# A routed expert layer on one core: room for 608 rows per expert in place of 640

## The chip, the cores and the metric

The kernel runs on one core of a Trainium2 chip. The metric is the time of one execution on the device in microseconds (us). A profiled execution has a span as well, from its first to its last instruction, and it is always a little shorter than that execution's time. TensorE (PE) multiplies, VectorE (DVE), ScalarE (ACT) and GpSimd (POOL) work on rows of 128 partitions, and SyncE (SP) issues most of the transfers.

## The reference

Three layers follow each other on 2304 tokens of width 512.

```python
# 1: attention through 32 memory slots, 4 x 8 heads, 576 tokens, head size 64 -> x (2304, 512)
# 2: mixture of experts, N, D, E, F = 2304, 512, 8, 1024
top2 = np.argpartition(-noisy_logits, 2, axis=1)[:, :2]
...
for e in range(E):
    for k in range(2):
        mask = top2[:, k] == e
        h = np.maximum(x[mask] @ w1[e], 0.0)
        out[mask] += top2_w[mask, k, None] * (h @ w2[e])
# 3: x @ w_in -> g = h * cos(h) -> g @ w_out, inner width 2048
```

Each token goes to two of the eight experts, so 4608 rows are spread over the experts, and how many each one gets depends on the inputs.

## The kernel before

**Stages.** The attention comes first, 18 tiles of 128 tokens. Then come the eight experts, one after the other, and then the last layer, again by tiles of tokens. All large products are made from pairs of half-precision numbers (a high part and a low part of each operand), so each product is three matmuls: high by high, high by low, low by high.

**Room.** Each expert has a fixed room of `CAP` = 640 rows, `NST` = 5 tiles of 128. The rows of the first eight token tiles (the first group, routed early) fill the first two tiles (`CA` = 2). All others go to the second group, tiles 2 to 4. When the first group gives an expert fewer than 256 rows, its two tiles are filled up, so the rows an expert uses are the larger of 256 and its first-group count, plus its second-group count. Rows that no longer fit are left to the function `overflow`, a loop over further tiles of 128 rows with a count `nov` that is computed on the chip (`slots_`). The loop reads the count from a register, stands between the first and the second product of the last expert, and runs zero times when every expert fits.

**One expert.** `gather_x` fetches an expert's rows from the table `xd` in DRAM, one indirect transfer for a tile of 128 rows (`xg`), and a transposing transfer puts them in `xT` (named x in the rows). `l1(e, part, f)` is the first product for block f of the inner width: 12 matmuls, whose moving operand is as wide as the part, 256 columns in the first and 384 in the second. `l1_out` writes the rectified result as high part on ACT and low part on DVE (hT). `l2(e, c)` is the second product for tile c: 24 matmuls with a piece of hT as stationary operand and 512 columns of weights moving. `l2_out` scales the tile on ACT (o) and stores it in the table `yd`. Expert 7 makes its products in another order than the rest: first part, tiles 0 and 1, second part, tiles 2 to 4.

**Work beside the experts.** The 16 weight matrices (index 2e and 2e + 1 for expert e) are loaded as f32 (raw), squared and summed on ACT (junk) for a scale, and split into high and low parts (w) on ACT and DVE. The weights of the last layer arrive as 64-bit floats in 16 chunks, are converted on DVE and ACT (cvt, cvu), and stored to `wst` in DRAM, from where `load_win` and `load_wout` read them back. The column sums for the scales are small matmuls on PE (sums).

**Order.** A planner writes everything in one list, `line`. Each entry has a planned time, and the list is sorted by it and issued. `put_l1` and `put_l2` advance a planned clock by `d1` and `d2` and note when ACT and DVE have room (`free`). `put_weights` and `put_chunk` take the next free slots, first come first served. Instructions of one engine keep the order in which they were issued (`chain`), and a second list (`settle`) does the same for the last layer, planned back from `m0`, the end of the expert stage.

Of the kernel before, what the change touches and what calls it, by code (L numbers as in the profile page):

```python
# [11 lines left out]
F32 = mybir.dt.float32  # L12
# [4 lines left out]
AF = mybir.ActivationFunctionType  # L17
OP = mybir.AluOpType
# [3 lines left out]
P = 128  # L22
# [3 lines left out]
DM = H * D  # L26
E = 8
F = 1024
DFF = 2048
CAP = 640  # L30
NST = CAP // P
GROUPS = [(0, 8), (8, 18)]
NA = GROUPS[0][1]
NG = NT - NA
ROUTE_OF = [g for g, (a, b) in enumerate(GROUPS) for t in range(a, b)]
CA = 2
MAXOV = 26
Y0 = MAXOV * P
YROWS = Y0 + E * CAP
TB = N // 4  # L40
# [22 lines left out]
def fused_kernel(ctx, tc, phiT, qT, kv, wgn, noise, w1, w2, wi, wo, out):  # L63
    nc = tc.nc
    V, A, G, T, SP = nc.vector, nc.scalar, nc.gpsimd, nc.tensor, nc.sync

    xd = nc.dram_tensor("xd", (N, 2 * DM), F16).ap()
    yd = nc.dram_tensor("yd", (YROWS, DM), F32).ap()
# [99 lines left out]
    def l2k(shape, dt, name):  # L168
        return lp.tile(shape, dt, tag="l", name=name)
# [27 lines left out]
    ecap = sm([P, E], F32, "ecap")  # L197
    G.iota(ecap, pattern=[[CAP, E]], base=0, channel_multiplier=0, allow_small_or_imprecise_dtypes=True)
    ekey = sm([P, E], F32, "ekey")
# [83 lines left out]
    def chain(key, fn, *a, **kw):  # L283

        with gated(key):
            last[key] = fn(*a, **kw)  # L286
# [87 lines left out]
    ne = base[1]  # L374
# [8 lines left out]
    def rt(name, shape, dt=F32):  # L383
        return small.tile(shape, dt, tag="r" + name, name="r" + name)
# [139 lines left out]
    def slots_():  # L524

        ti = rt("oi", [P, E], I32)
        cnt = rt("ocnt", [P, E])
        V.tensor_scalar(cnt, ne, float(-CAP), 0.0, op0=OP.add, op1=OP.max)
        V.tensor_scalar(ti, cnt, 127.0, None, op0=OP.add)
        V.tensor_scalar(ti, ti, 7, None, op0=OP.arith_shift_right)  # L530
        V.tensor_copy(cnt, ti)
        ca, cb = rt("oca", [P, E]), rt("ocb", [P, E])
        V.tensor_copy(ca, cnt)
        for s in (1, 2, 4):
            V.tensor_copy(cb[:, :s], ca[:, :s])
            V.tensor_tensor(cb[:, s:], ca[:, s:], ca[:, :E - s], op=OP.add)
            ca, cb = cb, ca
        cinc, cexc = ca, rt("oce", [P, E])
        V.tensor_tensor(cexc, cinc, cnt, op=OP.subtract)
        V.tensor_copy(nov, cinc[:, E - 1:E])  # L540
        corr, corr4 = rt("ocorr", [P, E]), rt("ocr4", [P, E])
        V.scalar_tensor_tensor(corr, cexc, float(P), ecap, op0=OP.mult, op1=OP.subtract)
        V.tensor_scalar(corr, corr, float(-CAP - Y0), None, op0=OP.add)
        yield
        ge, sl = rt("g", [P, NT, E]), rt("ocm", [P, NT, E])
        pos = key
        V.tensor_scalar(corr4, ecap, -4096.0 / CAP, None, op0=OP.mult)
        V.tensor_tensor(pos, key, bc_e(corr4, NT), op=OP.add)
        V.tensor_scalar(ge, pos, float(CAP), None, op0=OP.is_ge)
        V.tensor_tensor(ge, ge, bc_e(corr, NT), op=OP.mult)  # L550
        V.scalar_tensor_tensor(sl, pos, float(Y0), bc_e(ecap, NT), op0=OP.add, op1=OP.add)
        V.tensor_tensor(sl, sl, ge, op=OP.add)
        yield
        sf = rt("osf", [P, NT, 2])
        for k in range(2):
            V.tensor_tensor(ge, sl, oh[k], op=OP.mult)
            V.tensor_reduce(sf[:, :, k], ge, axis=AX.X, op=OP.add)
        V.tensor_copy(sidx, sf)
        yield
        uf = rt("ouf", [P, MAXOV])  # L560
        G.iota(uf, pattern=[[1, MAXOV]], base=0, channel_multiplier=0, allow_small_or_imprecise_dtypes=True)
        cm = rt("ocm", [P, MAXOV, E])
        ef, of = rt("oef", [P, MAXOV]), rt("oof", [P, MAXOV])
        V.tensor_tensor(cm, bc_t(uf, MAXOV), bc_e(cinc, MAXOV), op=OP.is_ge)
        V.tensor_reduce(ef, cm, axis=AX.X, op=OP.add)
        V.tensor_tensor(cm, bc_t(uf, MAXOV), bc_e(cexc, MAXOV), op=OP.is_ge)
        V.tensor_tensor(cm, cm, bc_e(cexc, MAXOV), op=OP.mult)
        V.tensor_reduce(of, cm, axis=AX.X, op=OP.max)
        V.tensor_tensor(of, uf, of, op=OP.subtract)
        V.tensor_scalar(ef, ef, float(E - 1), None, op0=OP.min)  # L570
        V.tensor_copy(ue, ef)
        V.scalar_tensor_tensor(ua, ef, 32.0, of, op0=OP.mult, op1=OP.add)
        V.tensor_scalar(ua, ua, float(NST), None, op0=OP.add)

    slot_steps = slots_()

# [298 lines left out]
    def bank_y():  # L875
        return turns("y", (("kt", 1), ("ya", 0), ("yb", 0)))
# [6 lines left out]

    xT, hT, prod = {}, {}, {}
    parts = [(0, CA), (CA, NST)]

    xg = {}

# [16 lines left out]
        chain("load", SP.dma_start_transpose, out=xT[e, part][:, :, (c - c0) * P:(c - c0 + 1) * P], in_=xg[e, c])  # L905

    def l1(e, part, f):
        c0, c1 = parts[part]
        n = (c1 - c0) * P
        if f == 0:  # L910
            if part == 0:
                h = hs("hT", 0, [P, 2, 8, n], F16)
                hT[e, part] = h[:, 0], h[:, 1]
            else:
                hT[e, part] = tuple(hs("hT", 0, [P, 8, n], F16) for w in range(2))
        x = xT[e, part]
        ph = prod[e, part, f] = bank_h()
        w = wt[2 * e]
        for k in range(4):
            fs = slice(k * F + f * P, k * F + (f + 1) * P)  # L920
            with gated("rank" if f else f"t{NT - 1}P") if (e, part, k) == (0, 0, 0) and f in (0, 2) else nullcontext():
                chain("P", T.matmul, ph[:, :n], lhsT=w[:, 0, fs], rhs=x[:, k, :], start=(k == 0), stop=False)
            chain("P", T.matmul, ph[:, :n], lhsT=w[:, 0, fs], rhs=x[:, 4 + k, :], start=False, stop=False)
            chain("P", T.matmul, ph[:, :n], lhsT=w[:, 1, fs], rhs=x[:, k, :], start=False, stop=(k == 3))

    def l1_out(e, part, f):
        n = (parts[part][1] - parts[part][0]) * P
        hi, lo = hT[e, part]
        ph = prod.pop((e, part, f))
        chain("A", A.activation, hi[:, f, :], ph[:, :n], AF.Relu)  # L930
        with gated("m161") if (e, part, f) == (0, 0, 0) else nullcontext():
            chain("V", V.scalar_tensor_tensor, lo[:, f, :], ph[:, :n], 0.0, hi[:, f, :], op0=OP.max, op1=OP.subtract)

    def l2(e, c):
        part = 0 if c < CA else 1
        cs = slice((c - parts[part][0]) * P, (c - parts[part][0] + 1) * P)
        hi, lo = hT[e, part]
        w = wt[2 * e + 1]
        py = prod[e, c] = bank_y()
        for f in range(8):  # L940
            ws = slice(f * DM, (f + 1) * DM)
            chain("P", T.matmul, py, lhsT=hi[:, f, cs], rhs=w[:, 0, ws], start=(f == 0), stop=False)
            chain("P", T.matmul, py, lhsT=hi[:, f, cs], rhs=w[:, 1, ws], start=False, stop=False)
            chain("P", T.matmul, py, lhsT=lo[:, f, cs], rhs=w[:, 0, ws], start=False, stop=(f == 7))
# [17 lines left out]

    def l2_out(e, c):
        py = prod.pop((e, c))
        o = l2k([P, DM], F32, "o")
        chain("A", A.activation, o, py, AF.Copy, scale=ysc[:, e:e + 1])
        r0 = Y0 + e * CAP + c * P
        chain("A", A.dma_start, yd[r0:r0 + P, :], o)

    def overflow():  # L970

# [254 lines left out]
              zero[0][:, None, :].to_broadcast([P, 2, DM]))  # L1226


    d1, d2 = (1.31, 1.95), 5.18
    xe = 8 * sum(d1) + NST * d2  # L1230
    X = [a_end + 0.5]
    at(tA + 0.0094, next_pools)
    at(tA, gather_x, 0, 0, lead=LA)
# [153 lines left out]
    def put_weights(i, t_load, t_sq, t_hi):  # L1387
        for h in range(2):
            at(t_load[h], w_load, i, h)
        for c in range(4):  # L1390
            t_sq = slot(t_sq)
            at(t_sq, w_square, i, c)
        t = max(t_hi, put_scale(t_sq + 2.0, i, 4) + 1.5)
        for c in range(4):
            t = slot(t)
            at(t, w_hi, i, c)
            at(t + 1.2, w_lo, i, c)
# [3 lines left out]
    def put_chunk(c, t):  # L1401
        t = max(t, stored.get(c - 2, 0.0) + 4.0)
        at(t, c_load, c)
        t = slot(t + 9.0)
        at(t, c_abs, c)
        for k in range(4):
            at(t + 0.8 + 1.8 * k, c_bits, c, k)
        t = slot(t + 9.0)
        at(t, c_square, c)
        t = slot(put_scale(t + 2.0, 2 * E + c, 1) + 1.5)  # L1410
        at(t, c_hi, c)
        at(t + 1.2, c_lo, c)
        stored[c] = t + 4.0
        at(stored[c], c_store, c)

    OV, LP, PRE = 13.0, 16.0, 30.0
    x = X[E - 2]
    put_weights(2 * E - 1, (x + 12.0, x + 15.0), x + 27.0, 0.0)
    for c in range(2 * NCH):
        put_chunk(c, X[1] + 2.0 + 18.5 * c)  # L1420
    put_weights(2, (tA - 12.0, tA + 0.0001), X[0] + 1.0, 0.0)
    put_weights(3, (X[0] + 4.0, X[0] + 8.0), X[0] + 17.0, X[1] + 1.5)
    for e in range(2, E):
        x = X[e - 1]
        put_weights(2 * e, (x - 6.0, x - 3.0), x + 11.5, 0.0)
        if e < E - 1:
            put_weights(2 * e + 1, (x + 12.0, x + 15.0), x + 30.0, 0.0)
    for k in range(4):
        at(X[1] + 8.0 + 6.0 * k, slots)
    for u in range(0, MAXOV, 2):  # L1430
# [47 lines left out]
```

## Time and profile before

| | |
|---|---|
| median of 3 runs | 913.83 us (912.25 to 913.85) |
| the profiled execution | 912.87 us, span 911.1 us |
| mean granted TensorE clock | 0.977 of full speed |
| PE busy | 874.9 us, 96% of the span |
| DVE, ACT, POOL busy | 586.4, 468.8, 213.5 us |
| chain that ended last | PE 86%, DVE 4%, issue 4%, ACT 2%, DMA 2% |

The attention takes the first 105 us, the experts follow to 530 us, the last layer takes the rest. The chain that ended last is the profile's own path back from the last instruction, through whatever released each step. Idle time of an engine that is off that path costs nothing by itself.

### The profile page before, as it was taken

The page shows a single profiled execution, that of the slowest core. Times are in us where ns is not written, and L with a number is a line of the kernel's source. Part 1 is how long each engine was busy: PE and PEld are TensorE (multiplying, and loading weights), DVE is VectorE, ACT ScalarE, POOL GpSimd, SP SyncE. Part 2 cuts the span into 40 slices and gives each one's busy share as a digit, 9 for nine tenths or more (in the row PEclk, how much of TensorE's full clock was granted, in tenths as well). Part 3 has the DMA queues.
Part 4 walks back from the last instruction along what each step waited for, and adds up shares of the span by engine and source line. Part 5 has one row for each costly group of instructions (what it writes and reads, how often), then busy time and mean ns, then how long its engine had stood idle before and what let it go on. Part 6 is the DMA issues. An engine that isn't in the chain of part 4 may idle for free.

```text
span 911.1 us, 14175 instructions
## 1 busy us (share of the span) xinstructions
PE 874.9 (96%) x5368; PEld 509.5 (56%) x5368; DVE 586.4 (64%) x1267; ACT 468.8 (51%) x830; POOL 213.5 (23%) x234
## 2 busy tenths in 40 slices
PE   5997499999999999999999999999999999999997
PEld 4875355756556474656646566664444444444564
DVE  3668753776658575775762469999878645455564
ACT  4688426566666676777772344454433322322233
POOL 1355222110200101020000145442632222122221
PEclk9897599999999999999999999999999999999999
DMA  9982459887868979698656534240512102100001
GB/s 350 395 322 83 115 157 248 258 282 255 236 252 257 266 225 310 234 280 329 188 178 216 140 133 115 59 104 24 139 47 47 47 1 24 46 1 1 1 24 47
DMA packets 108406, 146.55 MB, mean 161 GB/s; under 512 B 65840, under 2 KB 66736, under 8 KB 106288
## 3 DMA queue, kind: packets, MB, share of 16 engines
q1 hardware_dynamic: 89840, 103.95, 37.0%
q0 software_dynamic: 6080, 19.93, 7.5%
q10 hardware_dynamic: 12416, 21.74, 6.6%
q8 instruction: 43, 0.70, 0.3%
q14 instruction: 27, 0.22, 0.1%
HBM read 95.26 MB, written 35.13 MB: 143 GB/s over the span
## 4 chain that ended last, share of the span: by engine, by line
PE 86%; DVE 4%; issue 4%; ACT 2%; DMA 2%; POOL 1%; ACTq 0%; SPq 0%; POOLq 0%; DVEq 0%
PE h L286 22%; PE y L286 22%; PE g L286 19%; PE o L286 18%; PE x L756 1%; DVE tt L286 1%; PE kp L656 1%; PE sc L726 1%; DMA kvt<-in_kv 1%; DVE ty L286 1%; ACT tt L286 1%; POOL xg L896 1%; DMA xg<-xd,idxB 0%; ACT o L286 0%; PE sums L286 0%
## 5 line engine op out<-in xcount | busy, mean ns | idle before, releaser
L286 PE MATMUL h<-x,w 128*128 128x384 f16 (+1 forms) x1536 | 215.1, 301 | 9.1 <-DMA x<-xg 8.7
L286 PE MATMUL y<-w,hT 128*128 128x512 f16 x960 | 210.5, 379 | 0.0
L286 PE MATMUL g<-x2T,win 128*128 128x256 f16 (+1 forms) x1152 | 202.2, 326 | 0.0
L286 PE MATMUL o<-wout,gT 128*128 128x512 f16 x864 | 201.5, 379 | 0.0
L286 PEld LDWEIGHTS <-w 128*128 128x128 f16 x1536 | 151.5, 99 | 68.0 <-DMA x<-xg 8.8
L286 PEld LDWEIGHTS <-win 128*128 128x128 f16 x1152 | 112.7, 98 | 83.9
L286 PEld LDWEIGHTS <-hT 128*128 128x128 f16 x960 | 93.9, 99 | 109.0
L286 POOL TENSOR_TENSOR gT<-ty,gT 128x256 f16<-128x256 f32 (+1 forms) x96 | 90.9, 947 | 246.2 <-ACT gT L286 246.0
L286 ACT ACTIVATE tt<-tt,hp 128x256 f32<-128x256 f32 (+1 forms) x96 | 59.0, 614 | 156.0 <-DVE tt L286 149.7
L286 PEld LDWEIGHTS <-gT 128*128 128x128 f16 x864 | 84.6, 98 | 91.8
L286 DVE SCALAR_TENSOR_TENSOR hT<-h,hT 128x384 f16<-128x384 f32 (+1 forms) x128 | 61.6, 486 | 77.4 <-ACT hT L286 77.2
L286 DVE SCALAR_TENSOR_TENSOR w<-raw,wsc,w 128x1024 f16<-128x1024 f32 x64 | 81.0, 1286 | 32.8 <-ACT w L286 32.7
L286 DVE SCALAR_TENSOR_TENSOR ty<-g,wis,bct 128x256 f32<-128x256 f32 (+1 forms) x96 | 58.8, 612 | 66.3 <-PE g L286 64.2
L286 ACT ACTIVATE hT<-h 128x384 f16<-128x384 f32 (+1 forms) x128 | 55.5, 435 | 75.9 <-PE h L286 72.5
L286 DVE SCALAR_TENSOR_TENSOR ty<-g,fac,tt 128x256 f32<-128x256 f32 (+1 forms) x96 | 59.0, 615 | 45.0 <-ACT tt L286 44.3
L286 ACT ACTIVATE gT<-ty 128x256 f16<-128x256 f32 (+1 forms) x96 | 50.2, 523 | 62.2 <-DVE ty L286 60.9
L896 POOL DMA_INDIRECT xg<-xd,idxB x24 | 25.4, 1058 | 218.2 <-DMA x<-xg 206.9
L286 ACT ACTIVATE w<-raw,wsc 128x1024 f16<-128x1024 f32 x64 | 71.7, 1140 | 4.7 <-ACT o L286 2.1
L286 DVE SCALAR_TENSOR_TENSOR tt<-tt,ty 128x256 f32<-128x256 f32 (+1 forms) x96 | 69.6, 725 | 3.0
L286 ACT ACTIVATE junk<-raw 128x1024 bf16<-128x1024 f32 x64 | 67.3, 1052 | 3.9 <-ACT o L286 3.4
L286 ACT ACTIVATE o<-y,ysc 128x512 f32<-128x512 f32 x40 | 27.5, 687 | 67.3 <-PE y L286 66.2
L286 POOL DMA_INDIRECT y<-yd,sidx x36 | 35.2, 979 | 86.5 <-DMA yd<-o 79.3
(235 smaller groups left out, 710.2 us busy)
## 6 DMA issues: line engine op xcount, KB each, us to landing
raw<-in_w SPq DMA_DIRECT2D x32, 1024.0 KB, 8.7
yd<-o ACTq DMA_DIRECT2D x40, 256.0 KB, 5.6
kvt<-in_kv SPq DMA_DIRECT2D x9, 1024.0 KB, 15.5
cvt<-in_wi SPq DMA_DIRECT2D x8, 1024.0 KB, 6.5
wst<-cvt SPq DMA_DIRECT2D x16, 512.0 KB, 3.6
cvt<-in_wo SPq DMA_DIRECT2D x8, 1024.0 KB, 8.8
yd<-zero ACTq DMA_DIRECT2D x13, 512.0 KB, 5.4
xd<-hl SPq DMA_DIRECT2D x18, 256.0 KB, 2.0
```

Of the source, the lines that this page charges most:

```text
L286: last[key] = fn(*a, **kw)
L656: T.matmul(kp[32 * j:32 * j + 32, g, :], lhsT=es[i][:, 32 * h:32 * h + 32], rhs=kvv[:, :, h * D:(h + 1) * D], start=(i == 0), stop=(i == 4))
L726: T.matmul(sc[p0:p0 + n, 64 * c:64 * c + 64], lhsT=qt[t // 8][:, c, c0:c0 + n], rhs=bdkt[b][:, c, :], start=True, stop=True)
L756: last[f"t{t}P"] = T.matmul(x[pn, g, 0:272], lhsT=eT[:, g, pn], rhs=bdv[b][:, g, :], start=True, stop=True)
L896: G.indirect_dma_start(out=g, out_offset=None, in_=xd[0:NA * P] if part == 0 else xd, in_offset=bass.IndirectOffsetOnAxis(ap=idx[:, col:co ...
```

## The change

The room becomes 608 rows: still five tiles, of which the fifth has 96 rows. The first product of the second group moves 352 columns in place of 384, its two output steps work on 352 columns, the second product of tile 4 has 96 stationary columns, and its output and store have 96 rows. Gathers and transposes keep all 128 rows of a tile. An expert with more than 608 rows hands its whole fifth tile, and all beyond, to the loop (`FULL` = 512), for which room is made for 28 tiles in place of 26. The planner is told of 1.80 us for a block of the second group in place of 1.95, it spaces the 16 chunks 17.8 us apart in place of 18.5, and the second weights of expert 7 take their slots after all other weights and chunks, no longer before.

```diff
-CAP = 640
-NST = CAP // P
+CAP = 608
+NST = -(-CAP // P)
+FULL = (NST - 1) * P
...
-MAXOV = 26
+MAXOV = 28
...
-        V.tensor_scalar(cnt, ne, float(-CAP), 0.0, op0=OP.add, op1=OP.max)
-        V.tensor_scalar(ti, cnt, 127.0, None, op0=OP.add)
+        V.tensor_scalar(ti, ne, float(P - 1 - FULL), 0.0, op0=OP.add, op1=OP.max)
         V.tensor_scalar(ti, ti, 7, None, op0=OP.arith_shift_right)
         V.tensor_copy(cnt, ti)
+        V.scalar_tensor_tensor(cnt, ne, CAP + 0.5, cnt, op0=OP.is_ge, op1=OP.mult)
...
+    width = (CA * P, CAP - CA * P)
...
     def l1(e, part, f):
-        c0, c1 = parts[part]
-        n = (c1 - c0) * P
+        n = width[part]
...
-        x = xT[e, part]
+        x = xT[e, part][:, :, :n]
...
     def l1_out(e, part, f):
-        n = (parts[part][1] - parts[part][0]) * P
+        n = width[part]
...
     def l2(e, c):
         part = 0 if c < CA else 1
-        cs = slice((c - parts[part][0]) * P, (c - parts[part][0] + 1) * P)
+        m = min(P, CAP - c * P)
+        cs = slice((c - parts[part][0]) * P, (c - parts[part][0]) * P + m)
...
-        py = prod[e, c] = bank_y()
+        py = prod[e, c] = bank_y()[:m]
...
     def l2_out(e, c):
         py = prod.pop((e, c))
-        o = l2k([P, DM], F32, "o")
-        chain("A", A.activation, o, py, AF.Copy, scale=ysc[:, e:e + 1])
+        m = min(P, CAP - c * P)
+        o = l2k([P, DM], F32, "o")[:m]
+        chain("A", A.activation, o, py, AF.Copy, scale=ysc[:m, e:e + 1])
         r0 = Y0 + e * CAP + c * P
-        chain("A", A.dma_start, yd[r0:r0 + P, :], o)
+        chain("A", A.dma_start, yd[r0:r0 + m, :], o)
...
-    d1, d2 = (1.31, 1.95), 5.18
+    d1, d2 = (1.31, 1.80), 5.18
...
-    x = X[E - 2]
-    put_weights(2 * E - 1, (x + 12.0, x + 15.0), x + 27.0, 0.0)
     for c in range(2 * NCH):
-        put_chunk(c, X[1] + 2.0 + 18.5 * c)
+        put_chunk(c, X[1] + 2.0 + 17.8 * c)
...
+    x = X[E - 2]
+    put_weights(2 * E - 1, (x + 12.0, x + 15.0), x + 27.0, 0.0)
```

On ACT the place that changes most is the end of expert 6 and the start of expert 7. In the order before, these are its instructions from the first conversion of expert 7's second weights (w_4866, from raw_4612 and raw_4651); w_4776 are its first weights, o and the store to yd belong to tiles of expert 6, and hT 128x256 is expert 7's first product.

```order
L286 ACTIVATE w_4866<-raw_4612,wsc_113 128x1024
L286 ACTIVATE o_4870<-y_4829,ysc_115 128x512
L286 DMA yd<-o_4870 128x512
L286 ACTIVATE w_4866<-raw_4612,wsc_113 128x1024
L286 ACTIVATE w_4866<-raw_4651,wsc_113 128x1024 x2
L286 ACTIVATE o_4906<-y_4873,ysc_115 128x512
L286 DMA yd<-o_4906 128x512
L286 ACTIVATE junk_859,wmx_109<-cvu_4687 128x1024
L286 ACTIVATE w_4776<-raw_4438,wsc_113 128x1024
L286 ACTIVATE o_4938<-y_4909,ysc_115 128x512
L286 DMA yd<-o_4938 128x512
L286 ACTIVATE hT_4941<-h_4942 128x256
```

In the changed program the second weights are called w_4938, the first ones w_4777, and from their first conversion on ACT has this.

```order
L287 ACTIVATE w_4938<-raw_4613,wsc_113 128x1024
L287 ACTIVATE o_4941<-y_4906,ysc_115 96x512
L287 DMA yd<-o_4941 96x512
L287 ACTIVATE hT_4944<-h_4945 128x256
L287 ACTIVATE hT_4944<-h_4964 128x256
L287 ACTIVATE w_4938<-raw_4613,wsc_113 128x1024
L287 ACTIVATE hT_4944<-h_4979 128x256
L287 ACTIVATE w_4938<-raw_4652,wsc_113 128x1024
L287 ACTIVATE hT_4944<-h_4996 128x256
L287 ACTIVATE w_4938<-raw_4652,wsc_113 128x1024
L287 ACTIVATE hT_4944<-h_5013 128x256
```

Three of the four conversions of expert 7's second weights have moved from before its first product to between the blocks of it, and the last piece of its first weights no longer stands just ahead of expert 6's last tile.

On SP's queue the place is the end of the expert stage, behind the loop. In the order before: chl_5526 and chl_5573 are token tiles 0 and 1 of the last layer, x2T is where they are transposed to, and wout_5619 is the first half of the last layer's second weights.

```order
L286 DMA wout_5425<-wst 128x2x2048
L286 DMA wout_5427<-wst 128x2x2048
L286 DMA_TRANSPOSE x2T_5545<-chl_5526 128x8x128
L286 DMA_TRANSPOSE x2T_5545<-chl_5573 128x8x128
L286 DMA wout_5619<-wst 128x4x2048
```

The same place of the changed program, where tile 1 is chl_5589:

```order
L287 DMA wout_5426<-wst 128x2x2048
L287 DMA wout_5428<-wst 128x2x2048
L287 DMA_TRANSPOSE x2T_5546<-chl_5527 128x8x128
L287 DMA wout_5619<-wst 128x4x2048
L287 DMA_TRANSPOSE x2T_5546<-chl_5589 128x8x128
```

The transpose of token tile 1 now stands behind the large load of wout.

## Rows read from the trace of the kernel before

**Rows 1.** Stages: us; PE, PEld, DVE, ACT, POOL busy (instructions); PEclk, DMA share, GB/s.
```profile
105.10:162.15 57.05, 56.45 (x337) 33.19 (x338) 25.34 (x74) 24.81 (x43) 12.37 (x13) 0.95 0.70 198
214.90:530.30 315.40, 315.40 (x1924) 188.25 (x1923) 190.63 (x334) 197.48 (x311) 29.55 (x27) 1.00 0.77 241
530.30:911.10 380.80, 375.58 (x2033) 199.00 (x2031) 265.57 (x529) 142.86 (x248) 121.39 (x127) 1.00 0.18 47
```
**Rows 2.** PE's waits, longest in total first (us, times, longest).
```profile
PE h L286 <- DMA x<-xg: 8.7, 1, 8.7
...
PE h L286 <- DVE hT L286: 0.2, 1, 0.2
```
**Rows 3.** Groups of PE matmuls by shape: busy us, mean ns of one, idle before.
```profile
L286 PE MATMUL h<-x,w 128*128 128x384 f16 x768 | 127.1, 326 | 0.1
L286 PE MATMUL h<-x,w 128*128 128x256 f16 x768 | 88.9, 277 | 9.0 <-DMA x<-xg 8.7 <-DVE hT L286 0.2
```
**Rows 4.** PE's timeline, expert 2: start us, us, instruction, count.
```profile
214.90 10.64 PE L286 MATMUL h<-x,w 128*128 128x256 f16 x96
225.38 0.28 PE L286 MATMUL sums<-wmx,ones 128*128 128x2 f32 x2
225.52 15.76 PE L286 MATMUL h<-x,w 128*128 128x384 f16 x96
241.12 0.28 PE L286 MATMUL sums<-wmx,ones 128*128 128x5 f32 x2
241.26 5.34 PE L286 MATMUL y<-w,hT 128*128 128x512 f16 x24
246.44 0.28 PE L286 MATMUL sums<-wmx,ones 128*128 128x2 f32 x2
```
**Rows 5.** Groups of PE's weight loads by shape.
```profile
L286 PEld LDWEIGHTS <-hT 128*128 128x128 f16 x960 | 93.9, 99 | 109.0
...
L286 PEld LDWEIGHTS sums<-wmx,ones 128*128 128x128 f32 x64 | 11.5, 194 | 4.8 <-ACT junk L286 2.0
```
**Rows 6.** ACT's timeline in the second group of expert 6.
```profile
440.15 0.49 ACT L286 ACTIVATE hT<-h 128x384 f16<-128x384 f32 x1 [0.42 <-PE h L286]
...
442.10 0.49 ACT L286 ACTIVATE hT<-h 128x384 f16<-128x384 f32 x1 [0.42 <-PE h L286]
```
**Rows 7.** Groups of ACT and DVE by shape: weights, and the first group's output.
```profile
L286 ACT ACTIVATE w<-raw,wsc 128x1024 f16<-128x1024 f32 x64 | 71.7, 1140 | 4.7 <-ACT o L286 2.1 <-DVE wsc L286 1.9 <-issue 0.6
...
L286 ACT ACTIVATE hT<-h 128x256 f16<-128x256 f32 x64 | 24.3, 380 | 35.7 <-PE h L286 32.3 <-PE tab L500 3.4
...
L286 DVE SCALAR_TENSOR_TENSOR w<-raw,wsc,w 128x1024 f16<-128x1024 f32 x64 | 81.0, 1286 | 32.8 <-ACT w L286 32.7
...
L286 DVE SCALAR_TENSOR_TENSOR hT<-h,hT 128x256 f16<-128x256 f32 x64 | 26.5, 418 | 19.3 <-ACT hT L286 19.3
```
**Rows 8.** SP's and PE's timelines where the last layer begins, and x2T's transposes.
```profile
514.53 10.52 PE L286 MATMUL y<-w,hT 128*128 128x512 f16 x48
...
530.29 6.71 PE L286 MATMUL g<-x2T,win 128*128 128x256 f16 x60
...
L286 SPq DMA_TRANSPOSE x2T<-chl x2: 1232/1317/1402, 511.5 to 517.9; - x2
...
519.18 0.53 SPq L286 DMA_DIRECT2D wout<-wst  x1
```
**Rows 9.** Transfers from 494 to 560 us: count, KB each, us from issue to landing.
```profile
wout<-wst SPq DMA_DIRECT2D x1, 2048.0 KB, 9.3
...
x2T<-chl SPq DMA_TRANSPOSE x4, 3.2
```
**Rows 10.** Work like that of one turn of the loop.
```profile
raw<-in_w SPq DMA_DIRECT2D x32, 1024.0 KB, 8.7
...
xg<-xd,idxB POOLq DMA_INDIRECT x24, 6.7
...
L498 DVE TENSOR_SCALAR ohp<-iota_r,pf x36: 235/241/548, 86.2 to 118.9; 128x128 f16<-128x128 f16 x36
```

More of the change, by code (lines that the diff above doesn't have):

```diff
@@ L542, in slots_ @@
         V.scalar_tensor_tensor(corr, cexc, float(P), ecap, op0=OP.mult, op1=OP.subtract)
-        V.tensor_scalar(corr, corr, float(-CAP - Y0), None, op0=OP.add)
+        V.tensor_scalar(corr, corr, float(-FULL - Y0), None, op0=OP.add)
         yield
@@ L546, in slots_ @@
         pos = key
-        V.tensor_scalar(corr4, ecap, -4096.0 / CAP, None, op0=OP.mult)
+        V.tensor_scalar(corr4, ekey, 4096.0, -4096.0 * E, op0=OP.mult, op1=OP.add)
         V.tensor_tensor(pos, key, bc_e(corr4, NT), op=OP.add)
@@ L572, in slots_ @@
         V.scalar_tensor_tensor(ua, ef, 32.0, of, op0=OP.mult, op1=OP.add)
-        V.tensor_scalar(ua, ua, float(NST), None, op0=OP.add)
+        V.tensor_scalar(ua, ua, float(NST - 1), None, op0=OP.add)
     slot_steps = slots_()
@@ L1226, in clear @@
               zero[0][:, None, :].to_broadcast([P, 2, DM]))
-    d1, d2 = (1.31, 1.95), 5.18
-    xe = 8 * sum(d1) + NST * d2
+    d1, d2 = (1.31, 1.80), 5.18
     X = [a_end + 0.5]
```

## The prediction

> **What bounds the kernel now.** I read the stages first, then PE's waits, then PE's timeline, because the whole gain of this change can only come from PE.
>
> The stages [rows 1]: from 214.90 to 530.30 us PE is busy for 315.40 of 315.40 us at full clock, while DVE has 190.63 and ACT 197.48. PE is the limit of the expert stage, with a third of the time free on the other two. In the last stage PE has 375.58 of 380.80 us. A busy PE alone would not prove it, since a matmul that waits inside its pipeline could look busy, so the waits and the spacings come next.
>
> PE's waits [rows 2]: the long one, 8.7 us for the first transposed rows of expert 0, lies before the changed work begins. The other wait on the expert stage's list is 0.2 us for hT. From the first product on nothing holds PE up.
>
> The spacings [rows 4]: 96 matmuls of 256 columns take 225.38 - 214.90 = 10.48 us, 109.2 ns each. 96 of 384 columns take 241.12 - 225.52 = 15.60 us, 162.5 ns each. 24 of 512 columns take 246.44 - 241.26 = 5.18 us, 215.8 ns each. (The mean ns of the groups [rows 3] is the length of one pipelined matmul and not what one costs.) From 256 to 384 columns a column costs 53.3 / 128 = 0.416 ns, from 384 to 512 the same 53.3 / 128. The cost is a straight line in the columns that move, so time is set by the columns, and nothing else shows at these widths.
>
> **The change, part by part.**
>
> The first product of the second group. 768 matmuls [rows 3] move 352 columns in place of 384, 32 less. On the line a matmul costs 162.5 - 32 x 0.416 = 149.2 ns, 13.3 ns less, and 768 x 13.3 ns = 10.2 us go. Between the rows on either side the cost is bounded by 109.2 ns (a 256-column matmul) and 162.5 ns (no gain). 352 lies a quarter of the way down between two points of a line with the same slope on both sides, so I take the line's value. The upper bound, no gain, stays as a case.
>
> The second product of tile 4. 8 x 24 = 192 matmuls have 96 stationary columns, and still move 512. By the line they still cost 215.8 ns: zero gain, and this is why a fifth tile that is a quarter smaller saves only in the first product. The other side of it is the weight load. Loads of 128 columns of half-precision hT last 99 ns and vanish behind matmuls; the slowest kind of 128-column load in the stage, f32, lasts 194 [rows 5]. Both are below the 215.8 ns of the matmul that covers them, so I take zero. If the cover were gone, a load of 99 ns on 192 matmuls would be 19.0 us.
>
> On this the Trainium skill has a rule that speaks against the change: "TensorE: Matmul & The Clock Gate", section "Weight-path perf modes — Fast Weight Load (FWL) and DoubleRow", says that the fast weight load is on only when the number of weights is 128 and the type isn't FP32, and gives it about a factor of two. By that page 96 columns would lose it. As an estimate from it, 99 ns x 2 x 96/128 is 149 ns, under the 215.8 ns of the spacing, and the sum stays the same; no run here shows a 96-column load yet.
>
> Output steps. ACT's and DVE's work on a block shrinks with its width, but its time to do it shrinks too. In the second group ACT starts a block every 442.10 - 440.15 = 1.95 us, with 0.42 us idle [rows 6]. The new period is 12 x 149.2 ns = 1.79 us. That leaves 0.26 us idle even if hT keeps its 0.49 us. ACT stays behind PE without holding it.
>
> The second weights of expert 7. Three of their four conversions now stand between the blocks of its first product. That product lasts 96 x 109.2 ns = 10.48 us. The first piece is behind it already. For each of the others DVE makes one low part and one block, 1.286 + 0.418 = 1.70 us, and ACT one high part and one block, 1.140 + 0.380 = 1.52 us [rows 7]. Counted from the second block's end (2 x 1.31 = 2.62 us), plus ACT's first pair of 1.52, plus three of DVE's of 1.70, they are done at about 9.2 us, 1.3 us before the second product begins. And that product needs its fourth piece only after 18 of its 24 matmuls, 3.9 us on. I cost it at nothing; beyond 5.2 us of lateness it would cost one for one. All other conversions keep a whole group or several second products as cover.
>
> The queue of SP. The transpose of token tile 1 is now behind the load of wout. In the clock of before the second group of expert 7 ends at 514.53 [rows 8], and after the change 96 x 13.3 ns = 1.28 us earlier, at 513.25. Then wout's buffer is free and the load goes out. It takes 9.3 us to land [rows 9], so to 522.6. The transpose of tile 1 is issued at 517.9 [rows 8]. If it had to wait for all of wout, it would land 3.2 us [rows 9] after 522.6, at 525.8. The first product that needs it started at 530.29, now 529.01. 3.2 us are left. I cost it at nothing, and behind it wout itself comes earlier, not later, than before (519.18).
>
> The rest (one more instruction in the slots' arithmetic, 28 in place of 26 places in a few small ones, one more clearing transfer, chunks 0.7 us closer) is in the free third of DVE, ACT and the queues: nothing.
>
> The loop. The reference's inputs decide it. I counted the choices of its own draw (seed 0): with the first group filled to 256, the experts use 596, 581, 580, 569, 588, 569, 591 and 578 rows. The largest is 12 below 608. The loop runs zero times, as before.
>
> **Sum.** 912.87 us (the profiled execution, span 911.1 and 1.77 around it) - 10.2 = 902.6 us. The median of the runs is 913.83, 0.96 above that execution, which makes 903.6 for them. I say 903.1.
>
> **The rivals.** Most likely besides the forecast is that something with thin cover comes late. The thinnest are the 3.2 us of tile 1's transpose and the 5.2 us of expert 7's weights. For it: the load and the transpose share a queue, and the gathers of y run beside them. Against it: both covers are worked out with the full durations. It would take a delay of 4 to 7 us to show, and cost 1 to 4: 904 to 907 us. Chance 0.11.
>
> No change: the cost of a matmul falls in steps and not along a line, or something I do not see takes up the 10 us. Only the spacings at three widths speak against it. 912.9 us, chance 0.03.
>
> Slower, by the weight loads: the 96-column load isn't covered by the matmul ahead of it. All of it would be 192 x 99 ns = 19.0 us, 902.6 + 19.0 = 921.6 us. It decides from 10.2 us / 192 = 53 ns of each load on; below that it only eats into the gain. Against it: even the f32 loads of 194 ns fit. Chance 0.04. (The rule of the Trainium skill named above would act in this place.)
>
> Slower, by the loop: one expert over 608 rows. One turn builds an index column with 36 operations of 241 ns on DVE, 8.7 us, then gathers, 6.7 us, and loads two weight matrices in four transfers of 8.7 us each beside that [rows 10], all ahead of its products. At least 8.7 + 6.7 = 15.4 us, so 918 us or more. Chance 0.02.
>
> **How the numbers follow.** The forecast, 902.6 to 903.6 us, has 0.80. The lower end of the range is a slightly better line and a fast run, 901.2 us. Upwards it takes in the late-cover case nearly to its end, 906.0. A measurement can tell about 0.2%, 1.8 us, from no change. Faster: forecast, late cover, and a little of partly covered loads, 0.92. Within 0.2%: 0.03. Slower: 0.05.
>
> **What would show it.** The 96 matmuls of 352 columns should take 14.3 us from the first's start to the next instruction's. Tile 4's 24 should still take 5.18 us, and the weight loads of 96 columns should stay below 215 ns each. The last layer should begin about 10.2 us earlier, and from there on take the same time. PE should have no new wait from expert 1 to the end of the expert stage. I am wrong if PE's list of waits has a new entry for x2T, w or wout, if instructions of the loop appear, or if the spacing of tile 4 is above 216 ns.

## The result, and the profile after

The changed kernel takes 905.16 us (median of 4 runs, 903.27 to 906.57) against 913.84 us before: a ratio of 0.9911, with a 95% interval of 0.9899 to 0.9924. Run again beside three of its variants it took 903.99 us, a ratio of 0.9895 (0.9879 to 0.9912). It is about 1% faster, as forecast, and within the range. But 10.2 of 912.87 us would be a ratio of 0.9888, and the first interval does not reach so far. One to two microseconds are missing, and the experiments are mostly about them.

The profiled execution took 905.39 us with a span of 903.6. First the stages of the trace after, from the first product of expert 2 to the last layer, and the last layer (columns as in [rows 1]):

```profile
213.44:522.78 309.34, 308.57 (x1923) 191.54 (x1922) 188.94 (x335) 196.27 (x312) 30.82 (x28) 1.00 0.79 248
522.78:903.60 380.82, 375.59 (x2033) 199.00 (x2031) 265.96 (x529) 142.84 (x248) 121.54 (x126) 1.00 0.18 45
```

Against [rows 1], expert stages 2 to 7 went from 315.40 to 309.34 us, 6.06 less where six times 1.28 us would be 7.7. PE is no longer busy for all of it: 0.77 us are idle. The last layer is the same, 380.82 against 380.80. It began 7.5 us earlier and not 10.2.

The groups of PE by shape, matmuls and then weight loads:

```profile
L287 PE MATMUL y<-w,hT 128*128 128x512 f16 x768 | 168.9, 379 | 0.5 <-DVE hT L287 0.3 <-ACT hT L287 0.2
...
L287 PE MATMUL h<-x,w 128*128 128x352 f16 x768 | 117.4, 312 | 0.0
...
L287 PE MATMUL y<-w,hT 128*96 128x512 f16 x192 | 42.8, 379 | 0.0
```
```profile
L287 PEld LDWEIGHTS <-hT 128*128 128x128 f16 x768 | 74.9, 98 | 88.4 <-DVE hT L287 0.8 <-ACT hT L287 0.7
L287 PEld LDWEIGHTS <-hT 128*96 128x96 f16 x192 | 23.2, 123 | 16.8
```

The 768 narrower matmuls and the 192 with 96 stationary columns are there. A load of 96 columns lasts 123 ns, longer than one of 128 columns with 98. Where the second products idle, they wait for hT, 0.46 us in all. PE's timeline from the last tile of expert 6 to the last layer shows the place (y is the second product, and pb a small matmul of the last layer that comes next):

```profile
465.86 5.36 PE L287 MATMUL y<-w,hT 128*96 128x512 f16 x24
471.06 8.02 PE L287 MATMUL h<-x,w 128*128 128x256 f16 x72
...
491.90 14.48 PE L287 MATMUL h<-x,w 128*128 128x352 f16 x96
506.22 4.70 PE L287 MATMUL y<-w,hT 128*128 128x512 f16 x21
511.11 0.60 PE L287 MATMUL y<-w,hT 128*128 128x512 f16 x2 [0.19 <-ACT hT L287]
511.98 5.57 PE L287 MATMUL y<-w,hT 128*128 128x512 f16 x25 [0.27 <-DVE hT L287]
517.38 0.38 PE L287 MATMUL pb<-ident,cmx 128*128 128x128 f32 x2
```

96 matmuls of 352 columns take 506.22 - 491.90 = 14.32 us, 149.2 ns each, to the digit what the line gave. The fifth tile takes 471.06 - 465.86 = 5.20 us. But the two tiles behind the second group take 517.38 - 506.22 = 11.16 us, where they took 524.89 - 514.53 = 10.36 before: 0.80 us are lost, twice at the last block of hT. (The two waits in brackets make only 0.46 us, because they count from the modelled end of the matmul ahead. What PE loses is read from the starts.) ACT's timeline shows what that block was behind:

```profile
506.70 0.80 ACT L287 ACTIVATE hT<-h 128x352 f16<-128x352 f32 x2
509.98 0.72 ACT L287 ACTIVATE chl<-y,cmx 128x512 f16<-128x512 f32 x1 [2.48 <-DVE cmx L287]
510.61 0.44 ACT L287 ACTIVATE hT<-h 128x352 f16<-128x352 f32 x1
```

The product of the last block ended at 506.4. Its output step stands in ACT's queue behind chl, the high part of token tile 1 of the last layer, and chl waits for VectorE (cmx, a scale for each row) until 509.98. The chain to chl starts from the stores of tiles 0 and 1 of expert 7. In the kernel before, the last hT stood behind the same chl. PE's and ACT's timelines of before:

```profile
498.93 15.76 PE L286 MATMUL h<-x,w 128*128 128x384 f16 x96
...
524.89 0.38 PE L286 MATMUL pb<-ident,cmx 128*128 128x128 f32 x2
```
```profile
515.42 0.72 ACT L286 ACTIVATE chl<-y,cmx 128x512 f16<-128x512 f32 x1 [2.13 <-DVE cmx L286]
516.05 0.85 ACT L286 ACTIVATE hT<-h 128x384 f16<-128x384 f32 x2
```

Counted from the first product of the group, chl started at 515.42 - 498.93 = 16.5 us before and starts at 509.98 - 491.90 = 18.1 us now. PE needs the last block after the group and 21 more matmuls, an estimate of 15.60 + 21 x 0.2158 = 20.1 us before and 14.32 + 4.53 = 18.9 us now. So two things met: chl came 1.6 us later, and the block was needed 1.28 us earlier.

A second place is in expert 5. PE's and ACT's timelines (sums is the small matmul for a scale, junk the square it needs, cvu the conversion of a chunk):

```profile
408.90 0.38 PE L287 MATMUL sums<-wmx,ones 128*128 128x2 f32 x2 [0.31 <-ACT junk L287]
```
```profile
398.20 1.17 ACT L287 ACTIVATE cvu<-cvt 128x1024 f32<-128x1024 f32 x1 [4.66 <-DMA cvt<-in_wo]
...
407.69 1.06 ACT L287 ACTIVATE junk<-cvu 128x1024 bf16<-128x1024 f32 x1 [0.42 <-DVE cvu L287]
```

A chunk's load lands late, ACT waits 4.66 us for it, and the square that PE waits for is late by the 0.31 us on PE's list. Expert 5 begins and ends with these rows of PE's timelines, before and after:

```profile
372.76 5.40 PE L286 MATMUL h<-x,w 128*128 128x256 f16 x48
...
425.43 6.71 PE L286 MATMUL h<-x,w 128*128 128x256 f16 x60
```
```profile
367.67 5.40 PE L287 MATMUL h<-x,w 128*128 128x256 f16 x48
...
419.65 6.71 PE L287 MATMUL h<-x,w 128*128 128x256 f16 x60
```

Because the attention stage ends between 104.8 and 107.0 us from one execution to the next, the experts are compared by their own lengths: from an expert's first product to the next one's, read off PE's timeline, for experts 1 to 7 (expert 0 is left out, since the granted clock differs in its first us: from 105 to 112 us it is 0.60 before and 0.52 after, a mean between half, 1.2 GHz, and full, 2.4 GHz, and PE had been busy for only 3.0 and 4.0 of the 15 us up to 105).

| kernel | expert 2 | expert 5 | expert 7 | 1 to 7 | against before |
|---|---|---|---|---|---|
| before | 52.67 | 52.67 | 52.19 | 368.00 | |
| changed | 51.56 | 51.98 | 51.72 | 360.69 | -7.31 |
| columns alone, 7 x 1.28 | 51.39 | 51.39 | 50.91 | 359.04 | -8.96 |

So 1.65 us of 8.96 are missing: 0.81 in expert 7, 0.59 in expert 5, 0.17 in expert 2, where two pairs of sums now stand behind each other. The other experts are within 0.03 us of the forecast.

The whole execution lacks more: it began its last layer 7.5 us earlier, 2.7 short of 10.2. Of these, 1.65 are the loss above, and 1.38 come from the attention stage, which ended at 106.52 us in place of 105.14. Expert 0 gave back 0.30, being 1.58 us shorter in place of 1.28. No run ties the attention's end to the change: the kernel with the width alone, below, ended it at 104.80 in one execution and at 106.66 in another.

### The profile page after: what moved, and what is told of

Its sections match the earlier page's. It is cut to its first block, busy times and chain, and to the rows that moved or that the text cites. A ratio compares the mean times of both kernels' runs of the same rounds, so it can differ in the third digit from the quotient of the medians.

```text
span 903.6 us, 14173 instructions
## 1 busy us (share of the span) xinstructions
PE 864.2 (96%) x5368; PEld 512.3 (57%) x5368; DVE 584.1 (65%) x1267; ACT 466.1 (52%) x830; POOL 213.5 (24%) x234
## 4 chain that ended last, share of the span: by engine, by line
PE 81%; DVE 7%; DMA 5%; ACT 3%; issue 2%; SPq 1%; POOL 0%; ACTq 0%; DVEq 0%; POOLq 0%
PE y L287 21%; PE g L287 19%; PE h L287 19%; PE o L287 18%; DMA ph<-in_phiT 2%; PE x L757 2%; DVE tt L287 1%; SPq L287 1%; DMA cvt<-in_wo 1%; DVE ty L287 1%; PE sc L727 1%; ACT tt L287 1%; PE kp L657 1%; DMA xg<-xd,idxA 1%; ACT o L287 1%
## 5 line engine op out<-in xcount | busy, mean ns | idle before, releaser
L287 PE MATMUL h<-x,w 128*128 128x352 f16 (+1 forms) x1536 | 205.5, 295 | 8.9 <-DMA x<-xg 8.6
L287 PE MATMUL y<-w,hT 128*128 128x512 f16 (+1 forms) x960 | 211.3, 379 | 0.5 <-DVE hT L287 0.3
L287 PEld LDWEIGHTS <-hT 128*128 128x128 f16 (+1 forms) x960 | 98.1, 103 | 105.2 <-DVE hT L287 0.8
L287 DVE SCALAR_TENSOR_TENSOR hT<-h,hT 128x352 f16<-128x352 f32 (+1 forms) x128 | 59.5, 471 | 79.6 <-ACT hT L287 78.7
L287 ACT ACTIVATE hT<-h 128x352 f16<-128x352 f32 (+1 forms) x128 | 53.7, 421 | 66.6 <-PE h L287 63.2
L287 ACT ACTIVATE o<-y,ysc 128x512 f32<-128x512 f32 (+1 forms) x40 | 27.4, 685 | 65.1 <-PE y L287 64.0
```

## The experiments

The theory: time falls by the columns that move and nothing else, less what comes late at places of thin cover. The rivals: the planner's new numbers have a part in the gain, the shorter fifth tile has one, or 96-column loads cost what is missing.

**Width alone, with the planner's numbers of before.**

```diff
-    d1, d2 = (1.31, 1.80), 5.18
+    d1, d2 = (1.31, 1.95), 5.18
...
-        put_chunk(c, X[1] + 2.0 + 17.8 * c)
+        put_chunk(c, X[1] + 2.0 + 18.5 * c)
```

with expert 7's second weights ahead of the chunks again.

> The 608-row room with the planner's numbers of before (1.95 us per block, chunks 18.5 us apart, expert 7's second weights ahead of the chunks). Theory 1 (the gain is the columns that move, 768 x 13.3 = 10.2 us, less what comes late where cover is thin): 96 matmuls of 352 columns take 14.32 us as in the changed kernel, the whole is 904 to 907 us, and since two hT of the last group now stand behind the last chl on ACT, PE waits for hT in expert 7 at least as long as in the changed kernel (0.46 us on its list there). Theory 2 (the planner's new numbers bring part of the gain): this run is over 907 us, with waits of PE in the experts that the changed kernel does not have.

It was faster than the changed kernel: 902.28 us, a ratio to before of 0.9884 (0.9867 to 0.9902). I had expected 904 to 907, with a longer wait for hT. Both of my theories were off: the planner's new numbers have no part in the gain but take something away. Of the 2.93 us between the two profiled executions (902.46 and 905.39), 1.72 are the attention stage, which ended at 104.80 us here. Experts 1 to 7 take 359.44 us in place of 360.69, and these 1.25 us are what the order costs. PE's timeline at the last block:

```profile
503.72 5.13 PE L287 MATMUL y<-w,hT 128*128 128x512 f16 x23
509.01 5.57 PE L287 MATMUL y<-w,hT 128*128 128x512 f16 x25 [0.17 <-DVE hT L287]
514.42 0.38 PE L287 MATMUL pb<-ident,cmx 128*128 128x128 f32 x2
```

514.42 - 503.72 = 10.70 us, 0.34 lost in place of 0.80. Two hT stand behind the last chl here, but chl itself comes earlier: it starts 16.8 us after the group's first product, and 18.1 us in the changed kernel, where one more hT stands ahead of it on ACT and on DVE. So of the 0.80 us, the narrower group alone costs 0.34, and the planner's numbers the rest.

**The planner's numbers alone, with 640 rows.** The same lines the other way, in the kernel before.

> The 640-row room with the planner's new numbers and the moved weights alone. Theory 1: PE does the same work and nothing comes late, 912 to 915 us, within 0.2% of before, and no wait for hT in expert 7 longer than 0.3 us because the group lasts 1.28 us longer. Theory 2 (the order itself is worth something): below 911 us.

913.72 us, a ratio of 1.0005 (0.9996 to 1.0015): no change, as the first theory had it. Expert 7 takes 52.20 us. chl starts as late as in the changed kernel, 18.4 us after the group's first product, and the last hT behind it is done at 19.5 us, but with 384 columns PE needs it only at 20.1. Expert 2 is 0.17 us longer, as in the changed kernel; the rest of the new order's cost appears only together with the narrower group.

**The fifth tile alone.**

```diff
-    width = (CA * P, CAP - CA * P)
+    width = (CA * P, (NST - CA) * P)
```

> The changed kernel with the first product of the second group back at 384 columns; only the fifth tile of the second product has 96 rows. Theory 1 (stationary columns cost nothing under 512 moving ones, although a load of 96 columns lasted 123 ns against 98 for 128): 24 matmuls in 5.18 to 5.20 us, 912 to 915 us. Rival (the shorter tile is what brings the gain, or what eats the missing 1.3 us of it): below 911 us, or above 916 us.

912.98 us, a ratio of 0.9996 (0.9986 to 1.0006). A fifth tile of 96 rows neither gains nor costs anything that can be measured in the time. With the first run this leaves the 32 columns as the whole gain.

**A room of 600 rows.** `CAP = 600`, all else as changed: 344 columns.

> The changed kernel with a room of 600 rows: 344 columns, 88 rows in the fifth tile. No expert has over 600 rows by my count (596), so the loop should not run. Theory 1 (time on a line in the columns): 768 x 8 x 0.416 ns = 2.6 us below the changed kernel, 902 to 903 us, 96 matmuls in 14.0 us. Rival (cost moves in steps of 32 columns, or late work eats what is won): the same time as the changed kernel within 1 us.

901.85 us, a ratio of 0.989 (0.9855 to 0.9926): with one of four runs at 906.59 the times tell little. The lengths tell more. Expert 6 takes 51.08 us in place of 51.41, 0.33 less, and 96 x 8 x 0.416 ns is 0.32. The line holds at 344 columns, which are no multiple of 32. In expert 7 the rival came true beside it:

```profile
507.45 0.61 PE L287 MATMUL y<-w,hT 128*128 128x512 f16 x2 [1.03 <-ACT hT L287]
508.32 5.57 PE L287 MATMUL y<-w,hT 128*128 128x512 f16 x25 [0.27 <-DVE hT L287]
```

The wait for the last hT grew from 0.46 to 1.30 us, and expert 7 takes 52.24 us, longer than before the change. The group is 0.32 us shorter here, so PE needs the block that much earlier. The rest is not the width: chl started 18.6 us after the group's first product (506.33 - 487.73) and not 18.1, because the gather (y) that its chain waits for landed later.

**The changed kernel and the width alone, once more.**

> The changed kernel once more, beside the other three on one chip. Theory (what it lacks of 10.2 us is 0.5 to 0.8 us of waiting for hT in expert 7, in every execution, and the wait for a square in expert 5 came from one late chunk load and not from the order): the wait for hT is there again, the wait in expert 5 need not be, and its time is 904 to 905.5 us. Rival (the wait in expert 5 belongs to the order): it is there again, with 0.3 us or more.

> The 608-row room with the planner's numbers of before, once more. Theory (those numbers order the last output steps better): 1 to 1.5 us below the changed kernel of the same call, expert 7 at 51.3 us in place of 51.7. Rival (the first comparison was scatter of the attention stage between executions): within 0.7 us of the changed kernel.

The changed kernel took 903.99 us, a ratio of 0.9895 (0.9879 to 0.9912), the width alone 902.71, a ratio of 0.9884 (0.9867 to 0.99). 1.3 us lie between them, again in the same direction. The lengths are surer than these medians, whose runs overlap: experts 1 to 7 take 360.98 and 359.44 us, and expert 7 of these 51.68 and 51.26. The wait in expert 5 was there a second time, now 0.64 us, so my view that a single late load had caused it no longer holds. PE's waits of this second execution, where the 1.9 belongs to the attention stage in all runs:

```profile
PE sums L287 <- ACT junk L287: 2.5, 2, 1.9
...
PE y L287 <- DVE hT L287: 0.3, 1, 0.3
```

**Output steps of the last group first.** In the changed kernel, expert 7's second group has its output steps one block earlier in the list:

```diff
-        at(x, l1_out, e, part, f)
+        at(x - (d1[part] if (e, part) == (E - 1, 1) else 0.0), l1_out, e, part, f)
```

> The changed kernel with the output steps of expert 7's second group one block earlier in the list, so that the last hT stands ahead of the second chl on ACT. Theory: no wait for hT in expert 7, which takes 50.9 to 51.0 us, and 0.5 to 1 us less than the changed kernel in all. Rival (chl and with it x2T become late): a new wait of the first g products for x2T, no gain.

902.83 us, a ratio of 0.9885 (0.9868 to 0.9901), 1.2 us under the 903.99 of the changed kernel. The wait for hT is gone, expert 7 takes 50.92 us, and no product waits for x2T. ACT's and PE's timelines:

```profile
505.80 0.80 ACT L287 ACTIVATE hT<-h 128x352 f16<-128x352 f32 x2
509.08 0.72 ACT L287 ACTIVATE chl<-y,cmx 128x512 f16<-128x512 f32 x1 [2.49 <-DVE cmx L287]
```
```profile
505.43 10.52 PE L287 MATMUL y<-w,hT 128*128 128x512 f16 x48
515.79 0.38 PE L287 MATMUL pb<-ident,cmx 128*128 128x128 f32 x2
```

10.36 us again, as before the change. So the 0.80 us of expert 7 are shown to come from the place of the last hT behind chl.

In this execution the wait in expert 5 was absent too, although the order there is the changed kernel's, so that part of the gain is not the edit's. SP's timelines tell why, first of the changed kernel's first execution, then of this one (cvt<-in_wo is the chunk's load):

```profile
379.56 8.07 SPq L287 DMA_TRANSPOSE x<-xg  x2
...
388.29 0.51 SPq L287 DMA_DIRECT2D cvt<-in_wo  x1
```
```profile
379.35 6.41 SPq L287 DMA_TRANSPOSE x<-xg  x2
...
386.42 0.50 SPq L287 DMA_DIRECT2D cvt<-in_wo  x1
```

The chunk's load left at 386.42 us, and at 388.29 and 388.45 in the two executions that waited, because the two transposes ahead of it held SP's queue for 6.41 us here and for 8.07 and 8.40 there. Counted from expert 5's first product these are 19.0 us here and 20.6 and 21.0 there; in the run with halved products below, which has the same order, it was 19.0 us, and again there was no wait. The order makes the cover of this chunk so thin that 2 us on the queue decide. Why the transposes held the queue longer is open.

**The same with 600 rows.**

> The same with a room of 600 rows, 344 columns. Theory: expert stage 425.15 - 768 x 40 x 0.416 ns (12.8 us) = 412.4 us, at most 413, with no wait for hT in expert 7; 900.5 to 901.5 us, the fastest so far. Rival (the narrower group takes the cover from something else): a new wait of PE of 0.5 us or more in the expert stage.

900.78 us, a ratio of 0.9871 (0.9854 to 0.9887), the fastest of all. The expert stage is 412.43 us against 425.15, 12.7 less, and 768 x 40 x 0.416 ns is 12.8. Part of this agreement is luck: expert 0 was 1.84 us shorter in place of 1.60, and experts 1 to 7 by 10.88 in place of 11.18. No wait for hT in expert 7:

```profile
487.58 14.16 PE L287 MATMUL h<-x,w 128*128 128x344 f16 x96
501.58 10.52 PE L287 MATMUL y<-w,hT 128*128 128x512 f16 x48
511.94 0.38 PE L287 MATMUL pb<-ident,cmx 128*128 128x128 f32 x2
```

**One turn of the loop.** `CAP = 592`.

> The changed kernel with a room of 592 rows: 336 columns, and by my count one expert (596 rows) over it, so one turn of the loop. Theory (the prediction's rival of the loop): the first products lose 768 x 16 x 0.416 ns = 5.1 us against the changed kernel, the turn adds 15.4 us or more between the first and second product of expert 7, all engines' instructions of the loop appear once, and the whole is 915 us or more, slower than before. Rival (the turn lies beside other work): under 911 us. If the count were wrong, no loop instruction, and 899 to 900 us.

944.97 us, a ratio of 1.0346 (1.0316 to 1.0376). The expert with 596 rows goes through the loop, and PE's second product of expert 7 is cut in two:

```profile
476.99 5.34 PE L287 MATMUL y<-w,hT 128*128 128x512 f16 x24
...
495.76 0.44 PE L990 MATMUL otab<-oha,ohp 128*128 128x1 f16 x2 [6.01 <-issue]
...
508.87 9.12 PE L1011 MATMUL h<-ox,owa 128*128 128x128 f32 x64 [8.52 <-DVE ox L1000]
517.83 7.03 PE L1016 MATMUL y<-owb,ohh 128*128 128x512 f32 x16
526.63 4.69 PE L287 MATMUL y<-w,hT 128*128 128x512 f16 x21 [1.77 <-PEq L978]
```

From the end of the first row (476.99 + 5.18 = 482.17) to 526.63 PE does nothing but this turn, 44.5 us. No other product of PE lies beside it. The bound of 15.4 us held, with a third of the price: the index column takes until 500 us since each one-hot row comes with a second operation on DVE and there is a pause of 6 us in issue ("issue" is time in which the engine waits for nothing that the profile shows; its cause is open), the gather and transpose take until DVE's sum at 508.1, and the products themselves take 16 us.

**The price of a load that isn't covered.** The second products of tiles 3 and 4 in halves of 256 moving columns:

```diff
-        for f in range(8):
-            ws = slice(f * DM, (f + 1) * DM)
+        n = DM // 2 if c >= NST - 2 else DM
+        for o in range(0, DM, n):
+            for f in range(8):
+                ws = slice(f * DM + o, f * DM + o + n)
...
```

> The changed kernel with the second products of tiles 3 and 4 made in two halves of 256 moving columns each: twice as many weight loads, each under a matmul half as long. Tile 3 has 128 stationary columns (loads of 98 to 99 ns), tile 4 has 96 (loads of 123 ns). Theory (a load costs nothing as long as it is shorter than the matmul that covers it): tile 3 takes 48 x 109.2 ns = 5.24 us, and tile 4, whose load of 123 ns is longer than 109.2 ns, 48 x 123 = 5.9 us or more. Rival (96 columns load no slower, the 123 ns are only how the record is drawn): tile 4 takes 5.24 us as well.

907.25 us in a single run, which by itself tells little. Tiles 1 to 4 of expert 2 on PE's timeline (24 + 24 matmuls of 512 columns, 48 + 48 of 256), the groups of the halved matmuls, and those of weight loads:

```profile
244.17 21.00 PE L287 MATMUL y<-w,hT 128*128 128x512 f16 x144
265.01 0.51 PE L287 MATMUL sums<-wmx,ones 128*128 128x2 f32 x4
```
```profile
L287 PE MATMUL y<-w,hT 128*96 128x256 f16 x384 | 43.3, 273 | 0.0
L287 PE MATMUL y<-w,hT 128*128 128x256 f16 x384 | 43.2, 273 | 0.0
```
```profile
L287 PEld LDWEIGHTS <-hT 128*128 128x128 f16 x960 | 93.7, 98 | 73.0 <-ACT hT L287 1.4 <-DVE hT L287 0.8 <-DVE cmt L287 0.5
L287 PEld LDWEIGHTS <-hT 128*96 128x96 f16 x384 | 41.7, 123 | 0.0
```

265.01 - 244.17 = 20.84 us, less 2 x 5.18 for the two whole tiles is 10.48 us for 96 matmuls, 109.2 ns each, and tile 4's groups are as busy as tile 3's. My expectation failed: loads recorded with 123 ns follow each other every 109 ns without holding a matmul. Their busy time, 41.7 us for 384, is 108.6 ns each and not 123, and no time is idle between them: their records overlap. The time is what the rival gave. Whether a load of 96 columns really takes longer, or only its record is longer, this run doesn't tell.

The wait for the last hT in expert 7 was 1.42 us in this run, with 352 columns as in the changed kernel. That gather had landed later again, and chl started 19.5 us after the group's first product (511.72 - 492.18).

## Why the prediction was right, step by step

**The time.** It lies in the range, but not where the forecast put its weight: 905.16 us is above the 902.6 to 903.6 that had a chance of 0.80, and inside the 904 to 907 of the late-cover rival, which had 0.11. The second measurement, 903.99, stands at the edge of that band. Some of the distance is luck of the execution, since 1.38 us of the profiled one are the attention's later end.

**What bounds the kernel.** Right. PE carried the whole gain, and the last layer took the same 380.8 us behind it.

**The columns.** Right to the digit: 149.2 ns predicted, 149.2 measured. Undisturbed experts became 1.25 to 1.27 us shorter, for 1.28.

**The fifth tile.** Right: 5.20 us against 5.18, nothing in the time of the run that changed it alone. The load became longer, 123 ns where 128 columns last 98 and the sum had used 99. The estimate from the Trainium skill's page "TensorE: Matmul & The Clock Gate" (section "Weight-path perf modes — Fast Weight Load (FWL) and DoubleRow") was 149 ns. The rule of the Trainium skill there, that fewer than 128 columns lose the fast load, fits the trace in its direction: three quarters of the columns take a quarter more time. The other runs bear it out: loads of 88 columns (600 rows) lasted 120 ns and of 80 (592 rows) 117, so a column costs about 0.4 ns below 128, and that line would reach about 135 ns at 128 columns, where 98 are recorded. The step at 128 is then a factor of about 1.4, an estimate from these records, where the prediction's estimate had taken two. The rival built on uncovered loads fell, even under 256 columns.

**Expert 7's second weights.** Right: its first product and tiles 0 and 1 take 491.90 - 471.06 = 20.84 us, and took 498.93 - 478.10 = 20.83. The conversions were done 8.6 us after the start, for 9.2 forecast.

**SP's queue.** Right that it costs nothing: wout left at 506.59, as the group ended, and the first g product had no wait.

**ACT behind PE, and the rest at nothing.** This is the step that failed in size. I looked at ACT's share of a block (0.26 us idle forecast, 0.29 measured in expert 6) and not at what stands between the blocks of the last group. The late-cover rival was the right kind of cost with the wrong places, and its price, 1 to 4 us, holds the loss at its lower end: I named tile 1's transpose and expert 7's weights as the thinnest covers, and what gave way was the last hT of expert 7 behind chl (0.80 us, shown by the run that moved it ahead) and a square in expert 5 (0.59 us, which goes with the time of a chunk's load in four executions of one order; no run changed that load alone). The terms put at zero measured 1.65 us in the first profiled execution and 1.94 in the second. I also expected PE to have no new wait, and it has three.

**The planner.** I counted the new numbers as neutral. Alone they nearly are (0.17 us in expert 2); with the narrower group they cost 1.25 and 1.54 us of experts 1 to 7 in the two comparisons. Which of the three (block time, chunk spacing, place of the weights) costs what was not separated.

**The loop.** Right that it does not run. Its price was bounded from below only, and is 44.5 us.

## What to carry to other kernels

Where PE is busy without a gap and time is a straight line in the moving columns, cut those columns, and expect nothing from fewer stationary ones. When a stage becomes shorter, look for chains that run beside it from a fixed start: a step of theirs that stands ahead of the stage's last output on an in-order engine holds that output, and every microsecond cut from the stage comes off the slack of that step. A room for uneven groups should be just above the largest group that occurs: the step from 608 to 600 rows is 2.6 us on the line and took 2.05 off the time with the outputs first, and a room that one expert does not fit costs 44.5 for the turn.

## What the runs showed that I had not expected

The attention stage, whose work none of the kernels changes, ended its part between 104.8 and 107.0 us after the start in the twelve profiled executions (that of before, that of after, and those of ten experiments). Between 20 and 30 us the granted clock was 0.50 to 0.56 in nine of them, most of that stretch at the lower level of 1.2 GHz, and 0.98 to 1.00 in three, at 2.4 GHz. PE's wait ahead of it was the same in both kinds (1.42 us before and 1.43 after, until 17.2 us). The executions with a full clock there were not the faster ones (105.14 us at 0.56 before, 106.52 at 0.99 after); after had its slower stretch later, 0.84 from 30 to 40 us, behind waits of PE of 0.85 and 1.74 us. Why is left open.
